# Re-annealing the table that orders an attention and feed-forward kernel, from the second batch on

## The chip, the cores and the metric

The kernel runs on one core of one Trainium2 chip. The metric is the device time of one execution in microseconds (us); a smaller time is better. The engines are called PE (TensorE, matmul), DVE (VectorE), ACT (ScalarE), POOL (GpSimd) and SP (SyncE, which here only issues transfers). PSUM has eight banks, which hold the results of matmuls.

## The reference

Eight batches of eight heads with 576 tokens of 64 go through linear attention with an exponential feature map; the result, 4608 tokens of 512, goes through a gated feed-forward layer.

```
phi(x):  p = x @ w_phi;  p = p - max|p|;  concat(exp(p), exp(-p))     # 128 -> 256 features
kv = sum_s phi(k)_s v_s ;  z = sum_s phi(k)_s
num / (phi(q) . z + 1e-6)   with  num = phi(q) @ kv
x = attention output as [4608, 512]
out = (relu(x @ w_gate) * (x @ w_val)) @ w_out                        # 512 -> 1536 -> 512
```

Inputs and output are float32; the products run in bfloat16.

## The kernel before

The whole kernel is one hand-made schedule. `ORDER` is a table of 2343 words. A word is `name.args:banks@slot`: the name of a step, its indices (batch or token group, chunk, head group), the PSUM banks that it uses and, where it opens a new buffer of a ring, which one. The last loop of the kernel walks the table and calls `do_<name>` for each word. Each engine carries out the steps that are its own strictly in the order of the table; a step on another engine is met only through the data, banks and buffers that they share.

The steps that the prediction speaks of, by batch `b` (attention) or token group `g` (feed-forward; group `g` below 8 is the first 512 tokens of batch `g`, group 8 holds the 64 leftover tokens of all batches):

- `kr` (PE, line 592) projects a third of the keys, 24 matmuls; `kx` (DVE, line 696) takes the largest absolute value; `ke` (ACT, line 688) the exponentials; `kv` (PE, line 794) sums keys by values, in products of 65 columns; `kc` and `kd` copy it from PSUM, on ACT or on DVE.
- `vs`, `vo` and `vq` (POOL, lines 745, 757 and 773) scale the values for `kv`.
- `qt` (DVE) transposes queries, `qc` (PE, line 854) projects them, `qx` and `qe` are their maximum and exponentials.
- `nu` (PE, line 917) makes the numerators, 65 columns; `nt`, `nv` and `nr` (DVE, lines 938, 948 and 956) scale and add them and take the reciprocal of the denominator; `nx` (POOL, line 960, writes `xu`) multiplies by it: one step for each 128 tokens of a batch.
- `xt` (SP, line 992) is a transposing transfer from `xu` into `xTs` (group 8: `xTm`). There are four for each group, and a group's first value or gate product needs all four.
- `fv` and `fg` (PE, line 1097) are value and gate products of one chunk of 128 of the 1536 columns, four matmuls of 512 columns each; `va` or `vb` (ACT or DVE) copy the value, `ga` (DVE, line 1118) applies the gate and writes `h`.
- `ps` (POOL, line 1337) makes half sums of `h`, and `fw` (PE, line 1361, 12 products of 256 columns) is the output product, in a form with seven products in place of eight; `ys` to `y4` add its parts; `ow` and others write to memory.
- `xs` (POOL, line 1169), `fi` (PE, line 1194) and their helpers do the same for the first products of groups 7 and 8; `xs` adds the token sums that `fi` multiplies.
- Loads: `lk`, `lq`, `lm` and `ln` (keys, queries and their leftover tokens) are issued by POOL (lines 464, 496, 508 and 514) in its own order, between its compute steps. `lv` and `lw` (values) and `xt` are issued by SP.

Batches overlap: while group 1 goes through its value and gate products, batch 2 is in its numerators and batch 3 in its projections. There is one buffer for loaded queries (`qn`) and one for keys (`kn`), four of `xu`, three of `u` and of `r`.

Of the kernel before, what the change touches and what calls it, by code (L numbers as in the profile page):

```python
# [53 lines left out]
vq.1.0 kr.1.2:5037 vq.1.1 pb.0.3:4 qx.1.0.2:6 kx.1.2.0:5@mk5 qe.1.0.1.1:1 va.0.10:2@val3
qe.1.0.1.0:1 qe.1.0.2.0:6 kv.1.1:4 mt.0 wo.1 kx.1.2.3:7 qy.1.0:2 kc.1.1:4@kv1 fg.0.9:1
ke.1.2.0.0:5@kp0 qz.1.0:2@my1 kx.1.2.1:0 kx.1.2.2:3 ke.1.2.3.1:7 ku.2@kT3 vo.1.0@vs4 ke.1.2.1.1:0
kk.1.2.0@ek4 qu.1.0@mz0 vs.1.0.1 kk.1.2.1 ke.1.2.3.0:7 fv.0.8:6 ga.0.9:1 ke.1.2.0.1:5 fg.0.10:4
lv.2.0 fg.0.8:2 va.0.8:6@val2 wo.2 kt.2.1@kT2 vs.1.0.0 ke.1.2.1.0:0 ga.0.10:4 vo.1.2@vs1 qw.1.0@cq1
vs.1.2.0 kt.2.0 vs.1.2.1 ke.1.2.2.0:3 mc.0:7156 ga.0.8:2 nu.1.2.1:0 ke.1.2.2.1:3 mx.0.3:6 kv.1.0:4
# [1418 lines left out]
```

## Time and profile before

| | us |
|---|---|
| runs of the kernel, median of 3 | 360.89 (360.67 to 361.22) |
| the profiled execution | 360.87 |
| its span (first to last instruction) | 359.1 |
| PE, POOL busy within the span | 352.9, 325.6 |
| DVE, ACT busy | 312.9, 235.8 |

The busy times are those of the profiled execution. Its span is what the rows of the trace add up to; the rest of its time, 1.8 us, lies around it. In rows of the trace the first number is the start in us from the start of the span, the second is the time from the first start to the last end of the instructions that the row groups (xN says how many), then the engine, the line of the kernel, the operation and output<-inputs; in square brackets stands how long the engine was idle before it and for whom it waited. SPq and POOLq mean that the row is the issue of a transfer, not the transfer. In a row on issues of transfers the last number is the median from issue to landing.

### The profile page before, as it was taken

How to read it: one execution, taken by the hardware profiler on the slowest of the kernel's cores; microseconds unless marked ns; L12 is line 12 of the kernel's file. 1: busy time of each engine (PE TensorE's matmuls, PEld its weight loads, DVE VectorE, ACT ScalarE, POOL GpSimd, SP SyncE). 2: the span in 40 equal slices, each digit the busy share in tenths (PEclk: the TensorE clock that was granted, in tenths of full speed). 3: DMA queues.
4: the chain of work that ended last, by engine and by line, in shares of the span. 5: the costliest groups of instructions: out<-in, count | busy, mean ns of one | idle time of the engine just before them, and what ended most of it. 6: DMA issues, size and time to landing. Idle time of an engine off the chain costs nothing.

```text
span 359.1 us, 10076 instructions
## 1 busy us (share of the span) xinstructions
PE 352.9 (98%) x3876; PEld 222.2 (62%) x3876; DVE 312.9 (87%) x721; ACT 235.8 (66%) x564; POOL 325.6 (91%) x393
## 2 busy tenths in 40 slices
PE   8999999999999999999999999999999999999996
PEld 6678966445575656765576546666656566444684
DVE  5999999989999999999997999999898853898744
ACT  3999996986698869786897269656861424454310
POOL 8674988999999999976999589989999999999994
PEclk9999999999999999999999999999999999999999
DMA  7999999990947494369215980778300221600017
GB/s 124 257 198 204 164 199 159 180 164 7 178 68 157 53 157 95 68 127 135 58 39 105 158 136 2 176 107 103 62 0 16 45 59 25 227 0 2 0 31 206
DMA packets 90770, 38.16 MB, mean 106 GB/s; under 512 B 64226, under 2 KB 86370, under 8 KB 90722
## 3 DMA queue, kind: packets, MB, share of 16 engines
q0 software_dynamic: 33504, 15.03, 32.5%
q1 hardware_dynamic: 56754, 21.83, 27.7%
q10 hardware_dynamic: 464, 0.66, 0.8%
q8 instruction: 30, 0.49, 0.6%
q14 instruction: 18, 0.15, 0.1%
HBM read 37.81 MB, written 9.44 MB: 132 GB/s over the span
## 4 chain that ended last, share of the span: by engine, by line
PE 85%; DVE 8%; ACT 2%; DMA 2%; issue 1%; POOL 1%; SPq 0%; DVEq 0%
PE bank L1097 35%; PE bank L1361 18%; PE bank L1194 10%; PE bank L794 5%; PE bank L1224 4%; PE bank L917 3%; PE bank L592 2%; PE bank L854 2%; PE bank L1256 2%; ACT kp L688 2%; DMA w64f<-in_w_phi_dram 2%; DVE t L938 1%; DVE u L948 1%; DVE h L1118 1%; DVE mk L696 1%
## 5 line engine op out<-in xcount | busy, mean ns | idle before, releaser
L688 ACT ACTIVATE kp<-bank 128x384 bf16<-128x384 f32 x192 | 84.2, 513 | 16.6 <-DVE mk L696 7.4
L1097 PE MATMUL bank<-xTs,wv 128*128 128x512 bf16 x304 | 75.7, 379 | 0.0
L1097 PE MATMUL bank<-xTs,wg 128*128 128x512 bf16 x304 | 74.6, 379 | 0.0
L869 ACT ACTIVATE qp<-bank 128x512 bf16<-128x512 f32 x128 | 69.9, 627 | 6.5 <-PE bank L854 4.2
L1118 DVE SCALAR_TENSOR_TENSOR h<-bank,val 128x512 bf16<-128x512 f32 x90 | 60.5, 680 | 6.7 <-PE bank L1097 4.5
L1112 ACT CAST val<-bank 128x512 bf16<-128x512 f32 x59 | 35.1, 594 | 33.4 <-PE bank L1097 30.4
L745 POOL TENSOR_TENSOR vs<-vn,ek 128x780 bf16<-128x780 f32 (+2 forms) x40 | 53.8, 1366 | 0.8 <-ACT ek L705 0.4
L696 DVE TENSOR_REDUCE mk<-bank 128x3 f32<-128x384 f32 x96 | 49.1, 542 | 0.2
L960 POOL TENSOR_TENSOR xu<-u,r 128x512 bf16<-128x512 f32 x36 | 37.4, 1045 | 11.6 <-DVE r L956 11.5
L1361 PEld LDWEIGHTS <-h 128*128 128x128 bf16 x432 | 41.1, 98 | 10.0 <-issue 2.6
L1097 PEld LDWEIGHTS <-wg 128*128 128x128 bf16 x304 | 27.8, 98 | 30.2 <-issue 1.3
L1097 PEld LDWEIGHTS <-wv 128*128 128x128 bf16 x304 | 27.6, 98 | 27.3 <-issue 0.9
L877 DVE TRANSPOSE_TENSOR_REDUCE maxq<-bank 128x16 f32<-128x512 f32 x56 | 36.9, 690 | 0.1
L948 DVE TENSOR_TENSOR u<-bank,t 128x195 f32<-128x195 f32 (+1 forms) x108 | 32.9, 327 | 1.8 <-POOL xu L960 0.9
L1361 PE MATMUL bank<-wo,h 128*128 128x256 bf16 x260 | 32.5, 273 | 0.0
L1337 POOL TENSOR_TENSOR vs<-h 128x256 bf16<-128x256 bf16 x42 | 28.0, 671 | 3.7 <-DVE h L1118 3.6
L938 DVE TENSOR_TENSOR t<-bank,cq 128x195 f32<-128x195 f32 (+1 forms) x96 | 29.6, 326 | 1.9 <-PE bank L917 1.2
L917 PEld LDWEIGHTS <-qp 128*128 128x128 bf16 x512 | 23.1, 98 | 10.2 <-issue 0.5
L1337 POOL TENSOR_TENSOR h<-h,vs 128x256 bf16<-128x256 bf16 x44 | 28.6, 676 | 0.0
L1337 POOL TENSOR_TENSOR vs<-vs,h 128x256 bf16<-128x256 bf16 x42 | 28.0, 672 | 0.6
L1337 POOL TENSOR_TENSOR h<-h 128x256 bf16<-128x256 bf16 x42 | 27.9, 674 | 0.3
L917 PE MATMUL bank<-kv,qp 128*128 128x65 bf16 x512 | 26.0, 193 | 0.2 <-ACT kv L805 0.2
(156 smaller groups left out, 686.0 us busy)
## 6 DMA issues: line engine op xcount, KB each, us to landing
vn<-in_v_dram SPq DMA_DIRECT2D x24, 256.0 KB, 4.3
out_dram<-xTs SPq DMA_DIRECT2D x17, 256.0 KB, 3.0
kn<-in_k_dram POOLq DMA_DIRECT2D x7, 512.0 KB, 8.1
qn<-in_q_dram POOLq DMA_DIRECT2D x7, 512.0 KB, 8.0
out_dram<-obp SPq DMA_DIRECT2D x14, 256.0 KB, 2.6
wv<-in_moe_w_val_dram POOLq DMA_DIRECT2D x3, 512.0 KB, 9.4
wg<-in_moe_w_gate_dram POOLq DMA_DIRECT2D x3, 512.0 KB, 8.8
wo<-in_moe_w_out_dram POOLq DMA_DIRECT2D x3, 512.0 KB, 8.3
```

The costliest lines, as they stand in the source:

```text
L688: nc.scalar.activation(kp_of(3 * b + j)[:, i, s].rearrange("p n f -> p (n f)"), bank[bk[0]][:, 0 : 3 * F], AF.Exp, scale=(1.0, -1.0)[s],)
L696: nc.vector.tensor_reduce(mk_of(3 * b + j)[:, :, i], bank[bk[0]][:, 0 : 3 * F].rearrange("p (n f) -> p n f", f=F), axis=AX.X, op=ALU.max, ...
L745: nc.gpsimd.tensor_tensor(vs_of(3 * b + j)[:, s, 0:n].rearrange("p n i e -> p (n i) e")[:, :, 0:e], src[:, lo:hi].rearrange("p h i e -> p ...
L869: nc.scalar.activation(qp_of(4 * b + i)[:, s, 4 * hq : 4 * hq + 4].rearrange("p h m -> p (h m)"), bank[bk[0]], AF.Exp, scale=(1.0, -1.0)[s],)
L877: nc.vector.tensor_reduce((maxq0[:, i] if b == 0 else maxq)[:, :, i, 4 * hq : 4 * hq + 4].rearrange("p t h -> p h t"), bank[bk[0]].rearran ...
L917: nc.tensor.matmul(bank[bk[0]][:, E * n : E * (n + 1)], lhsT=qp_of(4 * b + i)[:, s, h, :], rhs=kv_of(b)[:, h, s, 0:E],)
L948: nc.vector.tensor_tensor(u_of(serial(b, i))[:, lo:hi], parts(bk, n)[:, :, 0], t_of(3 * serial(b, i) + g)[:, 0:n], op=ALU.add,)
L960: eng.tensor_tensor(xu_of(n).rearrange("p (h d) -> p h d", d=D), u_of(n)[:, :, 0:D], r_of(n).to_broadcast([P, H, D]), op=ALU.mult,)
L1097: nc.tensor.matmul(bank[bk[0]], lhsT=w[:, dc, P * f : P * f + P], rhs=xT(g)[:, dc, :], start=(dc == 0), stop=(dc == NDC - 1),)
L1118: nc.vector.scalar_tensor_tensor(h2_of(g, f), bank[bk[0]], 0.0, val_of(NFC * g + f), op0=ALU.max, op1=ALU.mult)
L1337: eng.tensor_tensor(sum_of(g, n, j), a, b, op=op)
L1361: nc.tensor.matmul(bank[bk[0]][:, col : col + HN], lhsT=x[:, P * u : P * (u + 1)], rhs=w, start=(n in (1, 5, 6) and u == us[0] and j == 0) ...
```

## The change

Only the table changes. Its first 297 words, up to 39.08 us of the profiled execution (batch 1's first value and gate products for group 0), are the same. Behind them the same steps stand in another order, with other banks and other ring buffers, found by annealing on a model in which transfers land later than the trace had them. Three copies from PSUM go from ACT to DVE and three others from DVE to ACT (three `vb` became `va`, three `kc` became `kd`). The transfers on SP (113 words) keep their order among themselves, and so do the loads on POOL (54 words). But POOL's loads stand at other places between POOL's compute steps. Two lines of the diff:

```
-qc.3.1:4305 qx.3.1.3:5 qx.3.1.0:4 vs.3.1.0@vs2 ps.1.4.3 lq.4.2 xt.2.2 kk.3.2.0 vq.3.0@vr0 ps.1.4.2
+nr.8.0@r0 ku.4@kT2 y3.1:2 xt.2.3 lq.4.2 xt.2.2 od.0.0 fv.2.2:4 qe.3.1.1.1:6 qe.3.1.1.0:6
```

POOL before, at the last two normalisations of batch 2 (line 960, `nx.2.3` and `nx.2.2`) and the q load of batch 4 (line 496):

```order
92 L960 TENSOR_TENSOR xu_135<-u_127,r_131 128x512
93 L960 TENSOR_TENSOR xu_136<-u_128,r_132 128x512
94 L1337 TENSOR_TENSOR h_152<-h_152 128x256 x4
95 L1337 TENSOR_TENSOR h_152<-h_152,vs_98 128x256
96 L745 TENSOR_TENSOR vs_99<-vn_75,ek_94 128x12x65
97 L1337 TENSOR_TENSOR h_152<-h_152,vs_98 128x256
98 L496 DMA qn_73<-in_q_dram 128x8x256
```

POOL now, at the same place:

```order
97 L960 TENSOR_TENSOR xu_135<-u_127,r_131 128x512
98 L1337 TENSOR_TENSOR h_152<-h_152 128x256
99 L960 TENSOR_TENSOR xu_136<-u_128,r_132 128x512
100 L496 DMA qn_73<-in_q_dram 128x8x256
101 L745 TENSOR_TENSOR vs_99<-vn_75,ek_93 128x8x65 x2
102 L773 TENSOR_TENSOR vr_102<-vm_76,ek_93 64x8x65
103 L1337 TENSOR_TENSOR h_152<-h_152,vs_98 128x256 x2
```

The seven pieces of compute between the second normalisation and the load have moved elsewhere; the load follows it at once.

DVE before, at the reciprocal that `nx.2.2` waits for (the last line 956 here; line 696 is the absolute maximum of batch 3's keys):

```order
150 L956 RECIPROCAL r_130<-u_127 128x8
151 L696 TENSOR_REDUCE mk_85<-bank_65 128x3
152 L948 TENSOR_TENSOR u_128<-bank_69,t_126 128x195
153 L938 TENSOR_TENSOR t_125<-bank_63,cq_116 128x195
154 L948 TENSOR_TENSOR u_128<-bank_66,t_124 128x130
155 L948 TENSOR_TENSOR u_128<-bank_63,t_125 128x195
156 L956 RECIPROCAL r_131<-u_128 128x8
157 L696 TENSOR_REDUCE mk_85<-bank_67 128x3
```

DVE now:

```order
149 L696 TENSOR_REDUCE mk_85<-bank_68 128x3
150 L956 RECIPROCAL r_130<-u_127 128x8
151 L696 TENSOR_REDUCE mk_85<-bank_63 128x3
152 L938 TENSOR_TENSOR t_125<-bank_64,cq_116 128x130
153 L938 TENSOR_TENSOR t_126<-bank_69,cq_116 128x195
154 L948 TENSOR_TENSOR u_128<-bank_64,t_125 128x130
155 L948 TENSOR_TENSOR u_128<-bank_69,t_126 128x195
156 L696 TENSOR_REDUCE mk_85<-bank_67 128x3
157 L956 RECIPROCAL r_131<-u_128 128x8
158 L696 TENSOR_REDUCE mk_85<-bank_70 128x3
```

Three of the absolute maxima now stand ahead of that reciprocal, where one stood.

POOL before, from the last two normalisations of batch 7 (line 960) to the first token sum (line 1169):

```order
259 L960 TENSOR_TENSOR xu_135<-u_129,r_132 128x512
260 L1337 TENSOR_TENSOR vs_100<-h_152 128x256
261 L960 TENSOR_TENSOR xu_134<-u_128,r_131 128x512
262 L1337 TENSOR_TENSOR vs_98<-vs_100,h_152 128x256
263 L1337 TENSOR_TENSOR vs_100<-h_152 128x256
264 L1337 TENSOR_TENSOR h_152<-h_152 128x256
265 L1337 TENSOR_TENSOR vs_100<-h_152 128x256
266 L1337 TENSOR_TENSOR vs_98<-vs_100,h_152 128x256 x2
267 L1337 TENSOR_TENSOR h_152<-h_152 128x256
268 L1169 TENSOR_TENSOR qT_108<-xTs 128x512
```

POOL now:

```order
266 L960 TENSOR_TENSOR xu_136<-u_128,r_132 128x512
267 L1337 TENSOR_TENSOR vs_100<-h_152 128x256
268 L1337 TENSOR_TENSOR vs_99<-vs_100,h_152 128x256
269 L1337 TENSOR_TENSOR h_152<-h_152,vs_97 128x256
270 L1142 TENSOR_TENSOR wv<-wv 128x512
271 L1337 TENSOR_TENSOR h_152<-h_152 128x256 x2
272 L1337 TENSOR_TENSOR vs_99<-vs_100,h_152 128x256
273 L960 TENSOR_TENSOR xu_135<-u_127,r_130 128x512
274 L1337 TENSOR_TENSOR vs_100<-h_152 128x256 x2
275 L1337 TENSOR_TENSOR h_152<-h_152 128x256 x2
276 L1337 TENSOR_TENSOR vs_99<-vs_100,h_152 128x256 x2
277 L1169 TENSOR_TENSOR qT_108<-xTs 128x512
```

The normalisation ahead of the last one has moved up: seven pieces lie between them, where one lay. Seven pieces lay between the last one and the token sum, and six do now.

More of the change, by code (lines that the diff above doesn't have):

```diff
@@ L54 @@
[L54 to L59, printed above, removed]
@@ new lines @@
+fg.1.6:1 qx.2.0.2:2 qx.2.0.0:5 fg.1.3:4 fv.1.4:3 ga.1.6:1@hs12 ga.1.3:4@hs15 ke.2.2.3.0:6
+kk.2.2.1@ek0 kk.2.1.0@ek1 ke.2.2.3.1:6 va.1.4:3@val1 kk.2.1.1 qe.2.0.2.0:2@qp0 qx.2.0.3:7
+qe.2.0.1.0:0 lq.3.2 lv.2.2 lw.2.1 od.0.2 od.0.3 mn.0.1:5 mn.0.0:1 mn.0.2:4 qe.2.0.3.0:7
+nt.8.0.0:1@t0 kk.2.2.0 nt.8.0.2:4@t1 nv.8.0.0:1@u2 kt.3.2@kT1 fv.1.8:6 fv.1.0:3 nv.8.0.2:4 tw.2.0
+vb.1.8:6@val2 qc.2.1:1074 qe.2.0.2.1:2 va.1.0:3@val3 qe.2.1.0.1:1 vq.2.0@vr1 qe.2.1.0.0:1 fg.1.0:2
+kt.3.1@kT2 vs.2.0.1@vs2 vs.2.0.0 vq.2.1 fv.1.11:6 qx.2.1.1:0 qx.2.1.2:7 qx.2.1.0:1 vs.2.2.0@vs0
@@ new lines @@
+nt.2.3.2:3@t3 lv.3.3 lw.3.0 qt.3.1@qT0 lv.3.1 nv.2.3.2:3@u0 kx.3.1.1:7@mk4 nt.2.2.1:2@t2 fg.1.1:5
+ga.1.1:5@hs5 kx.3.1.0:0 kx.3.1.3:1 fv.1.9:3 kx.3.1.2:4 fg.1.7:6 nu.2.3.1:5 nt.2.3.1:5@t1
+ke.3.1.1.1:7 kk.3.0.0@ek2 ke.3.1.1.0:7 nu.2.3.0:7 nt.2.3.0:7@t0 va.1.9:3@val2 ke.3.1.3.0:1 kk.3.0.1
+ke.3.1.2.1:4 fg.1.9:3 ga.1.7:6@hs6 nv.2.3.1:5 nv.2.3.0:7 ga.1.9:3@hs7 ps.1.3.2 ps.1.3.5 ps.1.2.5
+ps.1.2.4 nx.2.0@xu1 ps.1.1.1 ps.1.2.1 fw.1.1:1 ps.1.1.3 ps.1.2.3 ke.3.1.0.1:0 ys.1:1 nu.2.2.2:4
+nu.2.2.0:0 kr.3.2:6573 ke.3.2.3.1:3@kp3 ke.3.2.1.0:5 nr.2.3@r1 nt.2.2.2:4@t3 nv.2.2.1:2@u1
@@ new lines @@
+ps.2.1.5 ps.2.2.5 kx.4.2.0:3 ke.4.2.2.0:2@kp3 kx.4.2.1:4 fv.2.8:0 fg.2.6:6 vb.2.8:0@val1
+ga.2.6:6@hs0 fg.2.8:7 ga.2.8:7@hs4 fw.2.1:1 ku.5@kT2 mn.1.0:0 mn.1.1:6 kk.4.1.1 kt.5.0 mw.1@cm1
+kx.4.2.2:2 ke.4.2.3.0:5 ke.4.2.0.0:3 ps.2.1.0 ke.4.2.3.1:5 ps.2.1.2 ps.2.2.2 ke.4.2.1.1:4
+ke.4.2.1.0:4 ke.4.2.0.1:3 qc.4.0:5437 ys.2:1 fw.2.2:1 vs.4.0.0@vs0 nt.8.1.1:6@t1 nt.8.1.0:0@t2
+ps.2.2.0 nv.8.1.0:0@u0 ps.2.3.2 vs.4.0.1 ps.2.4.0 ps.2.3.0 qe.4.0.1.1:4@qp0 qx.4.0.0:5 qt.5.1@qT0
+qe.4.0.1.0:4 ke.4.2.2.1:2 qe.4.0.2.0:3@qp2 qx.4.0.2:3 qe.4.0.0.0:5@qp4 nv.8.1.1:6 qx.4.0.1:4
@@ new lines @@
+qx.4.0.3:7 fw.2.5:0 fw.2.6:2 yw.2:2 kv.4.0:6 fv.3.5:4 ps.2.3.5 vb.3.5:4@val2 qe.4.0.0.1:5 y2.2:1
+qe.4.0.3.0:7@qp3 qe.4.0.2.1:3 qe.4.0.3.1:7 kc.4.0:6@kv1 fw.2.7:2 mn.1.2:5 qc.4.1:1374 ps.2.4.3
+ps.2.4.1 vs.4.1.1@vs1 ps.2.4.5 ps.2.4.2 qe.4.1.3.0:4 kk.4.2.1@ek1 fv.3.0:6 va.3.0:6@val3 yz.2:2
+fw.2.4:2 nt.8.1.2:5@t0 y1.2:0 qx.4.1.1:3 ln.2.0 ps.2.4.4 vs.4.1.0 qx.4.1.2:7 qx.4.1.3:4 qx.4.1.0:1
+nv.8.1.2:5 kt.5.2@kT3 y3.2:2 qe.4.1.1.1:3 qe.4.1.1.0:3 qe.4.1.2.1:7 fv.3.6:6 fw.2.3:0 y4.2:0
+kk.4.2.0 qe.4.1.2.0:7 qe.4.1.3.1:4 va.3.6:6@val0 qe.4.1.0.0:1 kr.5.0:3574 vs.4.2.0@vs3
@@ new lines @@
+kx.5.1.3:0 nu.4.3.0:5 nt.4.3.0:5@t3 nv.4.3.0:5 nr.4.2@r0 ke.5.1.3.0:0 ke.5.1.3.1:0 fv.3.8:2 fg.3.2:1
+nu.4.3.2:5 ga.3.3:6@hs3 fv.3.7:0 va.3.7:0@val3 ps.3.1.5 ps.3.2.5 ke.5.1.2.0:7 vb.3.8:2@val1
+nt.4.3.2:5@t0 nv.4.3.2:5 kx.5.1.1:4 fg.3.8:6 ga.3.8:6@hs9 ow.2.2 kr.5.2:2504 fg.3.10:7
+ke.5.2.0.1:2@kp3 ke.5.2.0.0:2 ke.5.1.0.1:3 kx.5.2.1:5@mk4 ga.3.2:1@hs10 ga.3.10:7@hs13 fg.3.7:6
+fv.3.9:1 ke.5.2.2.1:0 ke.5.2.2.0:0 ke.5.2.1.0:5 ke.5.1.0.0:3 vq.5.0 ps.3.3.5 ke.5.2.1.1:5
+va.3.9:1@val1 fv.3.1:7 va.3.1:7@val2 ps.3.3.0 nx.4.2@xu2 vs.5.0.1@vs2 ga.3.7:6@hs15 vs.5.0.0
@@ new lines @@
+kx.5.2.2:0 kx.5.1.0:3 ps.3.1.4 ps.3.1.2 ps.3.2.2 ps.3.3.2 ps.3.3.4 kx.5.2.3:4 kk.5.1.0@ek3
+ke.5.2.3.1:4 nr.4.3@r1 kx.5.2.0:2 fg.3.1:6 qc.5.0:0531 ga.3.1:6@hs0 kk.5.2.0@ek4 ke.5.2.3.0:4
+ps.3.2.4 ps.3.1.1 qe.5.0.2.0:3@qp0 qe.5.0.3.1:1@qp4 qe.5.0.3.0:1 qx.5.0.1:5 fg.3.9:7 ga.3.9:7@hs2
+qe.5.0.1.1:5@qp2 qe.5.0.1.0:5 fw.3.1:2 qx.5.0.3:1 kt.6.0@kT2 kv.5.0:6 qx.5.0.0:0 kd.5.0:6@kv0
+qc.5.1:4715 qx.5.1.3:5 qx.5.1.2:1 ys.3:2 kk.5.1.1 qe.5.0.0.1:0@qp3 qe.5.0.0.0:0 fw.3.2:2
+qe.5.1.1.1:7 nx.4.3@xu1 ps.3.2.1 ps.3.1.3 ps.3.2.3 ps.3.3.1 qx.5.1.1:7 fw.3.6:6 qe.5.1.3.0:5
@@ new lines @@
+va.4.10:7@val2 qw.5.0@cq1 ke.6.0.0.1:1@kp0 ke.6.0.0.0:1 ps.3.4.2 nx.8.1@xu0 ps.3.4.1 ps.3.4.5
+vs.5.2.0@vs3 ps.3.4.3 ps.3.4.0 kx.6.0.3:0@mk0 vs.5.2.1 kv.5.2:7 kx.6.0.1:3 ke.6.0.1.1:3 ke.6.0.1.0:3
+ke.6.0.3.0:0 ke.6.0.2.0:2 ke.6.0.3.1:0 ps.3.4.4 fw.3.3:4 nu.5.3.0:3 kx.6.0.0:1 nt.5.0.0:5@t2
+ke.6.0.2.1:2 kd.5.2:7 nv.5.0.0:5@u2 nt.5.0.1:6@t1 nv.5.0.1:6 nu.5.0.2:1 nt.5.0.2:1@t3 y4.3:4
+fg.4.1:7 nu.5.1.1:5 nu.5.1.0:0 fv.4.7:6 ga.4.1:7@hs5 kx.6.0.2:2 fg.4.3:4 nu.5.3.1:7 kt.6.1@kT3
+nt.5.3.0:3@t0 nt.5.1.1:5@t2 nv.5.1.1:5@u1 fv.4.3:2 kk.6.0.1@ek5 va.4.7:6@val1 va.4.3:2@val3
@@ new lines @@
+nv.5.0.2:1 nr.5.0@r0 nt.5.1.0:0@t1 nv.5.3.0:3@u0 lk.7.3 nx.5.0@xu3 lm.7.0 nu.5.1.2:6 fg.4.0:5
+ga.4.3:4@hs8 nu.5.2.0:1 nu.5.2.1:2 fg.4.7:3 nu.5.3.2:4 nv.5.1.0:0 nt.5.2.0:1@t2 nt.5.1.2:6@t3
+nt.5.3.1:7@t0 nv.5.1.2:6 nt.5.3.2:4@t1 nv.5.3.1:7 nr.5.1@r1 lq.6.2 nx.5.1@xu2 ow.3.3 fv.4.11:0
+nu.5.2.2:6 va.4.11:0@val0 nv.5.3.2:4 lw.6.1 xt.5.0 lv.6.0 ow.2.1 lm.7.1 xt.5.1 lv.6.3 fg.4.10:7
+nv.5.2.0:1@u2 nr.5.3@r2 nx.5.3@xu1 xt.5.3 lv.6.1 lv.6.2 ga.4.7:3@hs11 nt.5.2.1:2@t3 nv.5.2.1:2
+nt.5.2.2:6@t0 ga.4.10:7@hs0 fv.4.9:4 nv.5.2.2:6 nr.5.2@r0 fv.4.0:1 vb.4.0:1@val3 ga.4.0:5@hs3
@@ new lines @@
+nt.7.3.2:5@t1 nu.7.1.2:3 fv.6.2:2 nv.7.3.2:5 ga.6.7:7@hs12 nt.7.2.0:0@t2 nt.7.1.2:3@t3 ps.5.2.5
+wt.2.1.0 ps.5.2.3 fw.5.6:1 nu.7.2.1:5 fv.6.8:7 nv.7.1.2:3 nv.7.2.0:0@u0 ps.5.4.0 ps.5.3.2
+wt.4.1.0@kp2 wt.4.0.0 ps.6.1.3@vs3 ps.6.3.3 ps.5.4.1 ps.5.4.4 ps.5.3.5 ps.5.3.3 nt.7.2.1:5@t1 mt.3
+nv.7.2.2:4 yw.5:1 ps.6.1.1 nv.7.2.1:5 nr.7.2@r0 fv.6.0:3 nu.7.0.0:0 vb.6.2:2@val3 nt.7.0.0:0@t3
+nx.7.2@xu1 ps.6.2.3@vs2 ps.5.4.5 nr.7.1@r1 nx.7.1@xu0 ps.5.4.2 wt.3.0.0 nr.7.3@r2 vb.6.8:7@val1
+nt.7.0.1:6@t2 fg.6.8:4 nu.7.0.2:5 nt.7.0.2:5@t0 fw.5.7:1 fw.5.5:2 fg.6.2:7 yz.5:1 nx.7.3@xu3
@@ new lines @@
+fi.0.5.1:4 fi.0.11.1:5 fi.0.10.2:0 ps.8.1.0 ps.7.1.1 ps.8.1.1 iq.0.10:6@u2 ia.0.5:46
+iv.0.10.0:7@val2 ga.8.10:0@hs11 fi.0.10.7:3 fi.0.4.7:1 ps.7.1.0 ps.8.3.2 ga.8.4:2@hs14 fi.0.5.5:7
+fi.0.5.2:4 fi.0.5.6:6 ia.0.11:50 iq.0.5:7@u0 iv.0.4.1:1@val0 fi.0.4.4:1 fi.0.11.5:2 ps.8.1.4
+ps.8.3.4 ps.8.2.4 ps.7.3.0 iv.0.10.1:3@val3 ga.7.4:1 ib.0.5:67 fi.0.5.3:7 ps.8.3.3 iv.0.5.0:7@val2
+ga.8.5:4@hs0 ps.8.2.1 ps.8.3.0 fi.0.5.7:6 fi.0.11.6:0 ib.0.11:01 iq.0.11:2@u1 fi.0.10.4:3 ps.8.3.1
+fi.0.11.2:5 fi.0.11.3:1 iv.0.5.1:6@val1 ga.7.10:3@hs4 ps.7.1.4 fw.8.1:7 ys.8:7 iv.0.11.0:1@val0
@@ new lines @@
+ga.8.11:5@hs5 ps.8.2.2 ps.8.1.5 ps.8.2.0 ps.8.2.5 fi.0.5.4:6 fi.0.11.7:0 fw.8.2:7 ga.7.5:6
+iv.0.11.1:0@val2 fi.0.11.4:0 fw.8.6:4 yw.8:4 ga.7.11:0@hs7 ps.8.3.5 ps.7.2.0 ps.8.4.0 ps.8.4.5
+ps.8.4.4 fw.8.5:2 fw.8.7:4 yz.8:4 fw.7.1:3 y1.8:2 fw.8.4:4 ps.7.1.5 ps.7.2.1 ps.7.2.4 ps.8.4.1
+ps.7.2.5 ow.5.1 fw.7.6:1 ps.8.4.2 y2.8:7 ys.7:3 ps.8.4.3 yw.7:1 y3.8:4 fw.8.3:2 y4.8:2 fw.7.2:3
+ps.7.3.2 ps.7.3.4 ps.7.3.1 ps.7.3.5 fw.7.7:1 fw.7.5.1:5 fw.7.5.0:6 ps.7.4.2 ps.7.4.1 ps.7.4.4
+ps.7.4.0 ps.7.4.3 ps.7.4.5 yz.7:1 fw.7.4:1 y1.7.0:6 y1.7.1:5 y3.7:1 fw.7.3.0:6 y4.7.0:6 fw.7.3.1:5
```

394 lines of the change are left out of this document (167 added, 227 removed).

## The prediction

> **What bounds the kernel now.** I read the page first (busy shares, the chain that ended last), then busy time by stretch, the waits, and then transfers and timelines around the places where the order moves a load.
>
> ```profile
> span 359.1 us, 10076 instructions
> PE 352.9 (98%) x3876; PEld 222.2 (62%) x3876; DVE 312.9 (87%) x721; ACT 235.8 (66%) x564; POOL 325.6 (91%) x393
> PEclk9999999999999999999999999999999999999999
> PE 85%; DVE 8%; ACT 2%; DMA 2%; issue 1%; POOL 1%; SPq 0%; DVEq 0%
> ```
>
> TensorE is busy for 98% at full clock, and 85% of the chain is its own. The next view cuts the span behind the first word that moves; column two is the length, then PE, weight loads, DVE, ACT, POOL with their counts.
>
> ```profile
> 58.25:109.91 51.66, 51.36 (x601) 29.20 (x599) 50.10 (x126) 41.35 (x104) 51.09 (x53) 1.00 0.83 125
> 109.91:154.40 44.49, 44.45 (x536) 27.72 (x533) 42.47 (x98) 34.56 (x82) 44.00 (x54) 1.00 0.64 106
> sum 316.16, PE 315.40 PEld 193.88 DVE 278.10 ACT 202.97 POOL 297.69; mean PE 45.06 PEld 27.70 DVE 39.73 ACT 29.00 POOL 42.53
> ```
>
> The sum row is 39.08 to 355.24 us, from the first moved step to the start of the last matmul. From 58 to 154 us POOL is as full as PE (95.1 of 96.2 us): two engines bound that stretch, and PE alone the rest.
>
> How much can any order win? The first three of these rows (of the chain) give undisturbed spacings: 0.216 us for a product of 512 columns, 0.030 for 65, 0.110 for 256. The other two (of PE's timeline) are a key and a query projection.
>
> ```profile
> 110.07 4.32 PE bank L1097 x20
> 222.18 1.52 PE bank L794 x50
> 339.71 15.82 PE bank L1361 x144
> 153.95 0.52 PE L592 MATMUL bank<-w,kT 32*128 32x128 bf16 x24
> 107.75 0.68 PE L854 MATMUL bank<-qT,w 32*128 32x512 bf16 x8
> ```
>
> Behind 39.08 us the order holds 824 products of 512 columns (178.0 us), 672 of 256 (73.9), 1136 of 65 (34.1), 19 key projections at 0.52 and some 0.03 of switching (10.5), 13 query projections at 0.68 (8.8), and small ones for which I estimate 7: 312.3 of the 316.2 us. So PE loses about 4 us there, and no order of these steps gains more: 357 us is the floor.
>
> **The change part by part.** The work is the same. Each of the 19 and 13 projections, the products and the copies has the duration of its row wherever it stands; three PSUM copies going each way between ACT and DVE cancel. What can change is only PE's 4 us of loss: what waits vanish and what waits come. I went through the order for each transfer that follows a POOL step, since the DMA words keep their order on SP and among themselves on POOL, while POOL's loads are moved against its compute.
>
> *The place where a load moves.* In the order before, the q load of batch 4 stands five pieces behind the normalisation of batch 2's last two tiles. In the new one it stands directly behind the last of them, so it starts when the transpose of that tile does. Rows of before:
>
> ```profile
> 104.34 2.56 SPq L992 DMA_TRANSPOSE xTs<-xu  x2
> 101.87 2.04 POOL L960 TENSOR_TENSOR xu<-u,r 128x512 bf16<-128x512 f32 x2
> 109.07 0.93 POOL L496 DMA_DIRECT2D qn<-in_q_dram  x1
> 109.91 1.89 PE L1097 MATMUL bank<-xTs,wv 128*128 128x512 bf16 x8
> qn<-in_q_dram POOLq DMA_DIRECT2D x1, 512.0 KB, 6.2
> ```
>
> The two normalisations end at 103.9, the last two transposes issue back to back from 104.34 (the second at about 105.7), the load at 109.07 (landing after 6.2), the first product of batch 2 at 109.91. The landing of the second transpose, asked for alone, is:
>
> ```profile
> xTs<-xu SPq DMA_TRANSPOSE x1, 2.4
> ```
>
> It landed at 108.1, 1.8 us ahead of its use, and the load was issued after that. Now what these transposes cost where a load was issued with them; the answers for 236.0 to 236.5 and 160.4 to 160.9 us, with the issues:
>
> ```profile
> qn<-in_q_dram POOLq DMA_DIRECT2D x1, 512.0 KB, 9.2
> xTs<-xu SPq DMA_TRANSPOSE x1, 7.5
> 236.41 1.23 SPq L992 DMA_TRANSPOSE xTs<-xu  x1
> 236.32 0.97 POOL L496 DMA_DIRECT2D qn<-in_q_dram  x1
> kn<-in_k_dram POOLq DMA_DIRECT2D x1, 512.0 KB, 8.4
> xTm<-xu SPq DMA_TRANSPOSE x1, 7.5
> 160.57 1.51 SPq L992 DMA_TRANSPOSE xTm<-xu  x1
> 160.76 0.95 POOL L464 DMA_DIRECT2D kn<-in_k_dram  x1
> ```
>
> Twice a load within 0.2 us of the transpose, twice 7.5 us in place of 2.4, and the load itself ends later still. A third, with the k load 3.4 us ahead of it (57.33 against 60.75), took 5.6:
>
> ```profile
> xTs<-xu SPq DMA_TRANSPOSE x1, 5.6
> 57.33 0.92 POOL L464 DMA_DIRECT2D kn<-in_k_dram  x1 [1.30 <-DVE t L938]
> 60.75 1.34 SPq L992 DMA_TRANSPOSE xTs<-xu  x1
> ```
>
> All of these happened where nobody needed the tile soon. In the new order PE meets it at once: the words ahead of batch 2's first value product are the same number of each kind as before (16 value, 16 gate, 24 numerator, 7 key and 5 query projections and so on), so PE arrives at about 109.9 again. The load may be issued up to 1 us ahead of the transpose, since SP first issues the transpose before it. DVE adds to that: the reciprocal that the normalisation waits for has moved behind two more absmax reductions, by 0.48 us each (five in 2.38 us):
>
> ```profile
> 102.27 0.16 DVE L956 RECIPROCAL r<-u 128x8 f32<-128x8 f32 x1
> 102.35 2.38 DVE L696 TENSOR_REDUCE mk<-bank 128x3 f32<-128x384 f32 x5
> ```
>
> So it ends near 103.3 to 103.8, the normalisation (1.0) near 104.4 to 104.9, and the transpose is issued between 105.0 and 106.2; I take 105.7, as before. Its latency lies between 2.4 (no effect) and 8.0 (7.5 and the spread of the twins). The nearest rows are the twins' 7.5; the twin at 236 had two more transposes behind it, and here only an output follows, and the same q load alone took 6.2 at 109 us, so I take 6.8. The tile is there at 112.5, and the product starts 2.6 us later than at 109.91. **Term one: +2.6**, from 0 (no effect) to +4.3 (106.2 and 8.0).
>
> [...]
>
> *What that delay gives back.* While PE stands, POOL works on, so what PE lost behind POOL from 109.91 to 154.40 us is gone. The stretch holds 108 products of 512 columns (23.3), 96 of 256 (10.5), 206 of 65 (6.2), 4 key (2.2) and 2 query projections (1.4) and by my estimate 0.5 of small ones: 44.1 of 44.49 us. **Term two: -0.4.** Of POOL's pieces ahead of the late products, two groups:
>
> ```profile
> L745 POOL TENSOR_TENSOR vs<-vn,ek 128x780 bf16<-128x780 f32 (+2 forms) x40 | 53.8, 1366 | 0.8 <-ACT ek L705 0.4
> L1337 POOL TENSOR_TENSOR vs<-h 128x256 bf16<-128x256 bf16 x42 | 28.0, 671 | 3.7 <-DVE h L1118 3.6
> ```
>
> If POOL's cover is gone instead, because its half sums need the late products, this is 0: ahead of the first of them stand six pieces of line 745 (1.37) and six half sums (0.67), 12.2 us of POOL's work, more than PE's delay.
>
> *A wait that goes.* The token sum of batches 6 and 7 waited on a transpose that SP issued late, being in others until 287.9:
>
> ```profile
> 290.56 1.16 POOL L1169 TENSOR_TENSOR qT<-xTs 128x512 bf16<-128x512 bf16 x1 [0.68 <-DMA xTs<-xu]
> 292.40 1.48 PE L1361 MATMUL bank<-wo,vs 128*128 128x256 bf16 x12 [0.22 <-POOL vs L1337]
> 293.72 1.47 PE L1361 MATMUL bank<-wo,h 128*128 128x256 bf16 x12
> 295.39 1.48 PE L1361 MATMUL bank<-kp,vs 128*128 128x256 bf16 x12 [0.20 <-POOL vs L1337]
> ```
>
> PE lost 0.22 there and 0.35 later (1.67 from 293.72 to 295.39, against 12 x 0.110 = 1.32). In the new order the normalisations of the two tiles whose transposes held SP stand further ahead, and six half sums (6 x 0.67 = 4.0 us) lie between the last normalisation and the token sum, more than an undisturbed 2.4. **Term three: -0.6**, from -0.6 to 0.
>
> *The rest.* From 154 to 290 us PE loses 1.2 us by the same count of spacings, in many small pieces. Nothing in the new order takes a known one away; I take 0, with 0.6 either way.
>
> Sum: +2.6 - 0.4 - 0.6 + 0 = +1.6 on the profiled execution. That took 360.87 us (span 359.1 and 1.8 around it), as good as the median of 360.89: **362.5 us**.
>
> **The rivals.** Two rows bear on them, one of the transfers (the median of all 28 of this form) and PE's longest wait on another engine behind 39 us.
>
> ```profile
> xTs<-xu SPq DMA_TRANSPOSE x28, 2.5
> PEld L1361 <- POOL vs L1337: 1.4, 4, 0.5
> ```
>
> (1) *The landing isn't late* (faster, the other side). If the transpose lands within 4.2 us, by 109.9, term one is 0 and the sum is -1.0, or -1.4 if POOL's stretch stays as good without PE's delay: 359.5 to 359.9. For it speaks that the 28 transposes of this form have a median of 2.5; against it, that all three near a load took 5.6 or more. It decides at a latency of 5.2 (109.9 + 1.0): below that the change gains. [...] (3) *PE's clock falls*. A PE that stands for 2.6 us or more might lose its clock for a while. Every slice of before shows 9, and the longest of PE's waits on another engine behind 39 us is 0.5, so no row prices it; if PE ran at half speed for as long as it had stood, it would lose 1.3 more: 363.8.
>
> [...] (4) *The change does nothing*: the moved steps are all covered and PE's losses only change places, 360.6 to 361.2; this would need term one near +1, and I count it with (2).
>
> **How the numbers follow.** My forecast (a late landing, 361.6 to 363.6) has 0.43; rival 3, and a landing or a new wait that is worse, 0.11; rivals 2 and 4 together 0.17; rival 1 has 0.29. A measurement of this kernel tells about 0.2%, 0.7 us, from no change. Slower than 361.6: 0.43 + 0.11 = 0.54. Within 360.2 to 361.6: 0.17. Faster: 0.29. Forecast alone: 361.6 to 363.6. The range takes in the middle of rival 1 (359.6) and most of rival 3: 359.6 to 364.6.
>
> **What would show it.** In the profile of the changed kernel: the transpose issued at 105 to 106.2 us lands after 6 to 8 us, and a row of PE at line 1097 near 112 carries a wait of some 2.5 us on a transfer of xu; POOL has idle time behind it or PE no more waits until 154; the token sum near 292 has no wait on a transfer; PE's clock is 9 in each slice. The prediction is wrong if that transpose lands within 4 us, if the load isn't in flight with it, or if a wait of a microsecond or more stands at a place not named here.

## The result, and the profile after

| | us |
|---|---|
| the changed kernel, median of 4 runs | 372.19 (370.53 to 374.71) |
| the kernel before, on the same chip, median of 4 | 360.78 (360.01 to 361.22) |
| ratio to before | 1.0325, 95% interval 1.026 to 1.0389 |
| profiled execution and its span | 374.71, 372.9 |

The change makes the kernel 11.4 us slower, not 1.6. The four runs of the changed kernel differ by 4 us, and their mean granted clocks (the share of its full clock that PE was given) differ with them: 0.979 in the 374.71 us run, 0.986, 0.988 and 0.995 in the 370.53 us run. The profile is that of the slowest, 13.8 us over the profiled 360.87 of before.

Of its page, the span, PE and its clock in 40 slices of 9.3 us, and the chain:

```profile
span 372.9 us, 10026 instructions
PE 355.2 (95%) x3827; PEld 223.2 (60%) x3876; DVE 312.3 (84%) x721; ACT 234.5 (63%) x564; POOL 325.7 (87%) x393
PEclk9999999999996999999999996999999999999998
PE 76%; POOL 7%; DMA 6%; issue 3%; DVE 3%; ACT 3%; SPq 1%; POOLq 0%; ACTq 0%
```

In before, each slice had clock 9 and PE was 85% of the chain. Now two slices have 6, and transfers and POOL are in the chain. PE's waits from 39 us on:

```profile
PE bank L1097 <- DMA xTs<-xu: 8.2, 3, 3.7
PE bank L794 <- POOL vs L745: 0.2, 1, 0.2
```

Three waits on transposes, 8.2 us; before had none. PE's timeline shows where (first value products of groups 2, 4 and 5), and the table by stretches gives the clock behind the two long ones (the column behind POOL's):

```profile
112.96 0.61 PE L1097 MATMUL bank<-xTs,wv 128*128 128x512 bf16 x1 [3.70 <-DMA xTs<-xu]
114.64 3.62 PE L1097 MATMUL bank<-xTs,wg 128*128 128x512 bf16 x8
189.67 1.02 PE L1097 MATMUL bank<-xTs,wv 128*128 128x512 bf16 x3 [0.77 <-DMA xTs<-xu]
225.16 1.89 PE L1097 MATMUL bank<-xTs,wv 128*128 128x512 bf16 x4 [3.68 <-DMA xTs<-xu]
...
113.06:119.60 6.54, 6.32 (x32) 2.62 (x34) 0.51 (x1) 2.79 (x6) 6.52 (x8) 0.59 0.43 113
225.27:231.90 6.63, 6.63 (x39) 3.35 (x39) 0.41 (x1) 2.51 (x6) 6.63 (x8) 0.56 0.01 2
```

Eight gate products took 3.62 us at 114.64; undisturbed, eight take 1.89 (a row of e1 below). With 0.59 and 0.56 of the clock granted, the two slow stretches lost 6.54 x 0.41 = 2.7 and 6.63 x 0.44 = 2.9 us. Each of these two windows takes in an edge at full clock. Cut finer, the granted clock is 0.50 from 111.6 to 118.4 and from 224.3 to 231.1 us, 6.8 us each time, and 1.00 right before and behind. It fell while PE stood, 2.3 and 2.8 us into the two waits. Waits and clock together: 3.70 + 3.68 + 0.77 + 2.7 + 2.9 = 13.75, about the 13.8 by which this execution is longer.

The place that the prediction named, as it came out (transfers first, then the issues on POOL and SP):

```profile
qn<-in_q_dram POOLq DMA_DIRECT2D x1, 512.0 KB, 9.5
xTs<-xu SPq DMA_TRANSPOSE x1, 7.1
...
105.70 0.94 POOL L496 DMA_DIRECT2D qn<-in_q_dram  x1
104.18 2.80 SPq L992 DMA_TRANSPOSE xTs<-xu  x2
```

The load was issued at 105.70, the second transpose at 105.79; the transpose took 7.1 us in place of 2.4, landed at 112.9, and PE's product started at once. The load landed later still, at 115.2. What was late was the transpose's completion and not its data: between 106.6 and 108.3 us SP's queue moved 512 packets and 0.13 MB, which is the whole tile (128 x 512 numbers of two bytes). From 108.3 to 111.0 it moved 26 packets of almost no bytes, while 651 of the load's went; of the 1040 that POOL's queue moved from 106.6 to 115.2, 979 had gone by 112.9.

The place that it did not name is at group 5: three loads of POOL stand between the normalisations of batch 5, and a fourth right ahead of them.

```profile
205.70 0.96 POOL L464 DMA_DIRECT2D kn<-in_k_dram  x1 [6.46 <-DVE t L938]
207.84 0.75 POOL L508 DMA_DIRECT2D km<-in_k_dram  x1
208.59 0.91 POOL L496 DMA_DIRECT2D qn<-in_q_dram  x1
210.69 0.75 POOL L508 DMA_DIRECT2D km<-in_k_dram  x1
...
214.10 5.47 SPq L992 DMA_TRANSPOSE xTs<-xu  x1
220.93 1.91 SPq L992 DMA_TRANSPOSE xTs<-xu  x1
...
xTs<-xu SPq DMA_TRANSPOSE x1, 9.6
xTs<-xu SPq DMA_TRANSPOSE x1, 8.0
```

The transposes issued at 210.8 and 214.1 took 9.6 and 8.0 us. The issue of the one at 214.1 held SP for 5.47 us in place of 1.3, so the last one, whose tile was ready at 216.6, was issued only at 220.93. In before the same k and q loads were issued at 193.1 and 194.8, six microseconds ahead of the first of these transposes, and the third one, issued at 208.8, took 3.1:

```profile
194.76 0.92 POOL L496 DMA_DIRECT2D qn<-in_q_dram  x1
xTs<-xu SPq DMA_TRANSPOSE x1, 3.1
```

### The profile page after: what moved, and what is told of

Read it like the earlier page. It is cut to its first block, busy times and chain, and to the rows that moved or that the text cites. A ratio compares the mean times of both kernels' runs of the same rounds, so it can differ in the third digit from the quotient of the medians.

```text
span 372.9 us, 10026 instructions
## 1 busy us (share of the span) xinstructions
PE 355.2 (95%) x3827; PEld 223.2 (60%) x3876; DVE 312.3 (84%) x721; ACT 234.5 (63%) x564; POOL 325.7 (87%) x393
## 4 chain that ended last, share of the span: by engine, by line
PE 76%; POOL 7%; DMA 6%; issue 3%; DVE 3%; ACT 3%; SPq 1%; POOLq 0%; ACTq 0%
PE bank L1097 28%; PE bank L1361 18%; PE bank L1194 10%; PE bank L794 4%; DMA xTs<-xu 4%; PE bank L1224 4%; PE bank L917 3%; ACT kp L688 2%; DMA vm<-in_v_dram 2%; PE bank L592 2%; POOL vs L1337 2%; PE bank L455 2%; PE bank L854 2%; POOL vs L745 2%; PE bank L1256 2%
## 5 line engine op out<-in xcount | busy, mean ns | idle before, releaser
L1097 PE MATMUL bank<-xTs,wg 128*128 128x512 bf16 x288 | 77.7, 393 | 0.7
L1112 ACT CAST val<-bank 128x512 bf16<-128x512 f32 x62 | 36.4, 595 | 55.7 <-PE bank L1097 39.6
L917 PE MATMUL bank<-kv,qp 128*128 128x65 bf16 x512 | 25.0, 193 | 0.3 <-ACT kv L805 0.2
```

What stands on the lines that cost most here:

```text
L917: nc.tensor.matmul(bank[bk[0]][:, E * n : E * (n + 1)], lhsT=qp_of(4 * b + i)[:, s, h, :], rhs=kv_of(b)[:, h, s, 0:E],)
L1097: nc.tensor.matmul(bank[bk[0]], lhsT=w[:, dc, P * f : P * f + P], rhs=xT(g)[:, dc, :], start=(dc == 0), stop=(dc == NDC - 1),)
```

## The experiments

Theory A: a POOL load that is in flight when a transpose is issued holds back its landing; PE, which needs the tile at once, stands; and where it stands as long as here (3.70 and 3.68 us) it loses its clock on top. Rival B: the tiles come late by the order of DVE and POOL, and the loads are innocent. Rival C: the clock falls for a reason of its own. In e1 to e4 the table fills fewer lines of the file, so their line numbers are 13 lower (12 in e4): L1084 and L1085 are line 1097.

**e1: the q load of batch 4 three POOL steps later.**

```
-xt.2.3 lq.4.2 xt.2.2
+xt.2.3 xt.2.2
...
-vq.3.0@vr0
+vq.3.0@vr0 lq.4.2
```

> The changed kernel with one word moved: the q load of batch 4 (lq.4.2) stands three POOL steps later, behind vq.3.0. Theory A (that load, in flight with the transpose xt.2.2, holds back its landing, and the idle PE then loses clock): xt.2.2 lands about 2.5 us after its issue, near 108.3; the wait of 3.7 us at fv.2.2 is gone, so is the slow clock behind it (2.6 us); some 366 us in place of 372.2. Rival B (tiles are late by the order of DVE and POOL, loads don't matter): the wait stays, 372. Rival C (the clock falls whatever PE waits for): the wait goes and the slow clock stays at that place, 368.5.

Measured: 366.64 us (ratio to before 1.016, 1.0119 to 1.0202), against 1.0325 for the changed kernel. The transpose, and PE at group 2 and at group 5:

```profile
xTs<-xu SPq DMA_TRANSPOSE x1, 2.4
...
109.47 1.03 PE L1084 MATMUL bank<-xTs,wv 128*128 128x512 bf16 x3
110.33 1.89 PE L1084 MATMUL bank<-xTs,wg 128*128 128x512 bf16 x8
218.60 1.76 PE L1084 MATMUL bank<-xTs,wv 128*128 128x512 bf16 x4 [3.23 <-DMA xTs<-xu]
```

At the first place the latency is back at 2.4, there is no wait, and PE runs at full speed (eight gate products in 1.89 us). The second place keeps a wait of 3.23 us, and the clock's mean is 0.62 from 218.5 to 223.0 us. B and C fail here: one moved load takes away wait and slow clock.

**e2: the q load of batch 6 earlier, where POOL stood idle.**

```
-ps.3.4.4
+ps.3.4.4 lq.6.2
...
-lq.6.2 nx.5.1@xu2
+nx.5.1@xu2
```

> The changed kernel with one word moved: the q load of batch 6 (lq.6.2) is issued ahead of the k load of batch 7 (lk.7.3), where POOL stands idle for 6 us, in place of between the normalisations of batch 5. Theory A: with one 512 KB load less in flight from 208 to 219 us, the transposes of batch 5 land in 3 to 5 us, the last by 221; the wait of 3.7 us at fv.5.8 and the slow clock behind it (2.6 us) go; some 366 us in place of 372.2. Rival B: the transposes stay late because nx.5.2 is late; 372. If the k load alone holds them back, the wait only shrinks, to about 2 us, and the clock stays up: 368.

Measured: 367.10 us (1.0179, 1.0148 to 1.021).

```profile
221.12 1.04 PE L1084 MATMUL bank<-xTs,wv 128*128 128x512 bf16 x4
223.48 0.28 PE L781 MATMUL bank<-vs,kp 128*128 128x65 bf16 x4 [0.46 <-POOL vs L732]
```

The wait of 3.68 is gone, with the slow clock; what stays is 0.46 us for the values of batch 6, whose loads share the same time. A k load is still there, and the transpose issued at 210.4 took 6.3 us. But the product that needs all four tiles started at 221.12 without a wait, in place of 225.16 behind one. B fails here too.

**e3: both moves.**

> Both moves together. Theory A: both waits and both stretches of slow clock go, about 13 us: 359 to 361.5, within 0.3% of the kernel before. Rival B: 372. If one wait only moves on to the next transpose, 363 to 366.

Measured: 362.82 us (1.0057, 1.0038 to 1.0075). From 372.19, e1 takes 5.6, e2 5.1 and both 9.4 of the 11.4 us; the two places add up to 10.7, so they are nearly independent. 2.2 us stay over before (360.64), more than the expectation had.

**e4: the early load in the kernel before.** The expectation speaks of a place behind ps.1.3.1. In the kernel that ran, the load stood directly behind nx.2.2, as in the changed kernel, and was issued at 103.77, ahead of both transposes.

```
-nx.2.2@xu3
+nx.2.2@xu3 lq.4.2
...
-ps.1.4.3 lq.4.2 xt.2.2
+ps.1.4.3 xt.2.2
```

> The kernel before with one word moved: lq.4.2 stands behind ps.1.3.1, so it is issued near 105.8 us, with xt.2.2 (105.7), in place of 109.1. Theory A: xt.2.2 lands after 7 us in place of 2.4, near 112.8; PE waits 2.9 us at the first value product of batch 2; later waits give back 0.4: 363.3 if PE keeps its clock, up to 365.5 if it loses it. Rival B: the transposes are as early as before, so nothing changes: 360.8.

Measured: 362.00 us over 10 runs (1.0047, 1.0023 to 1.007); nine lie between 361.2 and 363.2 at clocks of 0.998 to 1.0, one, the profiled one, has 365.23 at 0.993. Its rows, the last two transposes first:

```profile
xTs<-xu SPq DMA_TRANSPOSE x1, 8.4
xTs<-xu SPq DMA_TRANSPOSE x1, 7.4
...
112.71 0.61 PE L1085 MATMUL bank<-xTs,wv 128*128 128x512 bf16 x1 [2.20 <-DMA xTs<-xu]
...
112.80:117.00 4.20, 3.98 (x12) 1.56 (x14) 1.72 (x4) 2.31 (x5) 4.17 (x3) 0.61 0.14 31
```

One moved load, with nothing else changed, makes 8.4 and 7.4 us of 2.5 and gives PE a wait of 2.2. The second transpose was issued 1.5 us behind the load. Behind the wait the clock's mean was 0.61 from 112.8 to 117.0 us in this execution: six value products from 113.54 took 2.70 us, four gate products from 116.08 again 1.03. If it was 0.50 while it was low, that makes some 3.3 us (4.2 x 0.39 / 0.50, an estimate). The other nine were not traced, so how long PE waited in them isn't known; their clocks show no such loss. Their median is 361.9, 1.2 us over before, where the expectation had 2.5 for a kept clock. Whether their waits were shorter or later waits gave more back is open.

**e5: PE kept busy in the two waits.** The words are an idle-filler that the kernel already uses at its start.

```
-fv.2.2:4
+zz.28:4 fv.2.2:4
...
-fv.5.8:6
+zz.28:6 fv.5.8:6
```

> The changed kernel, and in each of its two long waits (ahead of fv.2.2 and of fv.5.8) PE does 28 products of zeros of 256 columns (3.1 us) into the bank that the next product overwrites; all else stays. Theory A1 (the idle PE is what costs the clock): the two transposes land as late as before and PE's next real product starts at the same time, but the clock stays up, so some 5 us of the profiled 374.7 go, to 369.5; every run near that, the scatter of 370.5 to 374.7 gone. Rival C (the clock falls for another reason, such as the transfers' load or heat): 372 with the same scatter. If the added products cost time themselves: over 372.

Measured: 370.30 us (1.0269, 1.0254 to 1.0284); the four runs lie within 369.66 to 370.89, at clocks of 0.997 and 0.998.

```profile
110.29 3.22 PE L455 MATMUL bank<-zero 128*128 128x256 bf16 x28
114.88 1.89 PE L1097 MATMUL bank<-xTs,wg 128*128 128x512 bf16 x8
...
113.00:119.00 6.00, 5.44 (x45) 2.91 (x45) 2.44 (x5) 3.83 (x8) 5.92 (x6) 1.00 0.49 149
222.00:229.00 7.00, 5.79 (x83) 3.49 (x83) 1.89 (x3) 3.47 (x8) 6.71 (x7) 1.00 0.00 0
```

At group 2 the last two transposes still took 4.8 us in the median, as in the changed kernel (2.5 and 7.1 there), and 3.6 us lie between PE's last real product and its next at 114.0. But the clock is 1.00 behind both waits, and the scatter shrinks from 4.2 to 1.2 us. The transfers are the same, so it is the idle PE that costs the clock here. With the clock kept the kernel is still 9.6 us slower than before (360.67). The added products save 1.9 us in the median, and 4.1 between the two profiled executions (374.71 and 370.60).

**e6: the normalisation nx.4.3 two steps earlier, on top of e3.**

```
-nr.4.3@r1
+nr.4.3@r1 nx.4.3@xu1
...
-nx.4.3@xu1 ps.3.2.1
+ps.3.2.1
```

> Both loads moved as in e3, and the normalisation nx.4.3 two POOL steps earlier (right behind its reciprocal). In e3 PE waited 0.69 us on the transpose of that tile at fv.4.4. Theory (what is left of the loss in e3, 2.2 us over the kernel before, is waits for tiles that come late by the order itself): xt.4.3 is issued 1.2 us earlier, the wait goes, 0.7 to 0.9 us less than e3: 362.0. Rival: POOL's displaced half sums make PE wait as long; 362.8.

Measured: 362.24 us (1.0044, 1.0029 to 1.0058); the interval overlaps that of e3. The profile shows the wait of 0.69 at fv.4.4 gone, and another in its place:

```profile
183.39 1.89 PE L1097 MATMUL bank<-xTs,wv 128*128 128x512 bf16 x7
84.02 0.28 PE L794 MATMUL bank<-vs,kp 128*128 128x65 bf16 x4 [0.86 <-POOL vs L745]
78.43 1.06 POOL L773 TENSOR_TENSOR vr<-vm,ek 64x520 bf16<-64x520 f32 x1 [1.06 <-DMA vm<-in_v_dram]
```

The second looks like a third collision: the q load of batch 3 (lq.3.2), issued at 71.7 here and at 74.03 in before, with a load of values whose issue holds SP from 69.39 to 72.14 in the changed kernel. POOL waited for the values until 78.4 here; in before they had landed at 75.0, 4.6 us behind their issue. It does not strike each time: in the profile of e7, with the q load at 71.45, POOL took them at 77.20 and nobody waited.

**e7: the loads of batch 6's values ahead of batch 5's transposes, on top of e6.**

```
-lw.6.1 xt.5.0 lv.6.0
+lw.6.1 lv.6.0 lv.6.3 lv.6.1 lv.6.2 xt.5.0
...
-xt.5.1 lv.6.3
+xt.5.1
...
-xt.5.3 lv.6.1 lv.6.2
+xt.5.3
```

> As e6, and the four loads of batch 6's values (lv.6.x) are issued ahead of batch 5's transposes on SP, right behind lw.6.1, in place of between them. Theory: the transposes then meet one k load only and xt.5.2 isn't held up on SP, and the values are there when POOL wants them, so the waits at fv.5.8 (0.4 to 0.6) and at kv.6.0 (0.5 to 0.8) go: 1.2 us less than e6, 360.8, level with the kernel before or better. Rival: the values themselves then collide with the k load, no change against e6.

Measured: 361.83 us over 12 runs (1.0032, 1.0009 to 1.0056), which the intervals don't tell from e6, and with a scatter from 359.63 to 364.25. The gain of 1.2 us that was expected isn't shown. Its profiled run is the fastest and has none of the waits at groups 4 and 5.

**e8: term three alone.** The kernel before, with one transpose of batch 7 issued ahead of an output and of its neighbour.

```
-ow.5.2 xt.7.3 xt.7.2
+xt.7.2 ow.5.2 xt.7.3
```

> The kernel before with one transfer moved on SP: xt.7.2, whose tile is ready before that of xt.7.3, is issued ahead of it and of an output. This measures term three of the prediction by itself. By the prediction: xt.7.0 is issued some 1.3 us earlier, the token sum doesn't wait, and PE gains 0.6 us: 360.0 against 360.6. Rival: the output products wait on POOL's half sums all the same, no change.

Measured: 359.48 us (0.997, 0.9959 to 0.998), all seven runs between 359.37 and 360.09.

```profile
289.11 1.15 POOL L1169 TENSOR_TENSOR qT<-xTs 128x512 bf16<-128x512 bf16 x1
291.39 1.48 PE L1361 MATMUL bank<-wo,vs 128*128 128x256 bf16 x12
294.02 1.47 PE L1361 MATMUL bank<-kp,vs 128*128 128x256 bf16 x12
```

In before, the three like rows (290.56, 292.40 and 295.39, in the prediction) carried waits; now none does. By the medians the gain is 1.2 us (360.67 to 359.48), twice what was expected, and this version is faster than both kernels.

**e9: the q load of batch 3 two steps later, on top of e7.**

```
-lq.3.2 tw.2.0 vq.2.0@vr1
+tw.2.0 vq.2.0@vr1 lq.3.2
```

> As e7, and the q load of batch 3 (lq.3.2) two POOL steps later, behind vq.2.0: near 74.1 us, as in the kernel before, in place of 71.4, where a load of values (lw.2.1) was still being issued. In e5 and e6 lw.2.1 landed at 78.3 in place of 75.4 and PE waited 0.9 to 1.3 us for POOL behind it; in the profile of e7 it did not, and the runs of e7 scatter from 359.6 to 364.3. Theory: that landing is the scatter; without it all runs lie near the lowest of e7, 359.6 to 360.3. Rival: the scatter has another cause and stays, median 361.8.

Measured: 360.62 us over 12 runs (1.0007, 0.9994 to 1.0019), from 360.03 to 361.83. The scatter shrinks from 4.6 to 1.8 us, close to the 1.6 of before measured beside it, and the median is level with before, but not in the range given. In the profiled execution (361.69 us) a wait on POOL's half sums is now the largest:

```profile
143.89 1.48 PE L1361 MATMUL bank<-kp,vs 128*128 128x256 bf16 x12 [0.82 <-POOL vs L1337]
```

Five moves (two loads at the large waits, one normalisation, one group of value loads, one more load) give the whole loss back. Each of the small three lies within the intervals of its neighbour, and only their sum, 362.82 to 360.62, is clear.

**e10: half of the load at the same place.**

```
-xt.2.3 lq.4.2 xt.2.2
+xt.2.3 lq.4.0 xt.2.2
...
-vq.3.1
+lq.4.1 vq.3.1
```

> The changed kernel with the q load of batch 4 in halves: heads 0 to 3 (256 KB) where the load stood, with xt.2.2, heads 4 to 7 three POOL steps later. If the transpose's landing waits for as much of the load as is in flight (theory A in its strict form): xt.2.2 lands 4 to 5 us after its issue in place of 7.1, the wait at fv.2.2 is 1 to 2 us in place of 3.7, the clock stays there; 367.5. If the second half delays it all the same: 7 us, no change, 372. If the mere presence of a POOL load costs a fixed 5 us: 372.

Measured: 368.50 us (1.0218, 1.0198 to 1.0238). Load and transpose, and PE:

```profile
qn<-in_q_dram POOLq DMA_DIRECT2D x1, 256.0 KB, 5.1
xTs<-xu SPq DMA_TRANSPOSE x1, 5.2
...
110.99 1.04 PE L1097 MATMUL bank<-xTs,wv 128*128 128x512 bf16 x4 [1.79 <-DMA xTs<-xu]
...
110.99:116.00 5.01, 5.01 (x41) 2.65 (x42) 3.21 (x6) 3.85 (x8) 4.86 (x5) 1.00 0.71 137
```

With half the load, the transpose took 5.2 us in place of 7.1, and the load 5.1; both were issued between 105.6 and 105.8, so they landed within some 0.3 us of each other. So the delay grows with the bytes of the load ahead, as far as two sizes show it. Behind the wait of 1.79 the clock was 1.00 in this execution. The second half stood behind five POOL steps and not three; in the changed kernel these end at 111.0, about when the transpose landed here. The time is 1 us above the expectation; the waits at groups 4 and 5 were still there.

**e11: the load one step later.**

```
-xt.2.3 lq.4.2 xt.2.2
+xt.2.3 xt.2.2
...
-vs.3.0.1@vs2
+vs.3.0.1@vs2 lq.4.2
```

> The changed kernel with the q load of batch 4 one POOL step (1.05 us) later, behind vs.3.0.1, so that it is issued near 106.8, 1 us behind xt.2.2. If the transpose only waits for what stands in the DMA engines ahead of it: it lands near 108.5 to 109 and the wait goes, 366.6 as e1. If the two share the engines from there on: 4 to 6 us, a wait of 1 to 2, 368 to 369. If the load counts as long as the transpose hasn't landed: 7 us, 372.

Measured: 367.66 us (1.0188, 1.0149 to 1.0227), level with e1 within the intervals. The load was issued between 107.2 and 107.4, the transpose between 106.3 and 106.5:

```profile
qn<-in_q_dram POOLq DMA_DIRECT2D x1, 512.0 KB, 8.3
xTs<-xu SPq DMA_TRANSPOSE x1, 2.4
```

The load issued some 0.9 us behind the transpose didn't touch it: 2.4 us, as without it. This is no test of two transfers that run together: in before, the first packets of this load show at 110.7 us, 1.6 us behind its issue at 109.07; by that they came near 108.9 here (an estimate), and the transpose had landed by then (106.5 and 2.4). That only what was issued ahead can delay a transfer isn't shown either: in e5 the values that SP began to issue at 69.3 to 69.5 landed after 9.1 us with the q load of batch 3 issued 2 us later (71.42), and after 6.5 in e9, with it at 73.94.

## Why the prediction was wrong

**Term one was right in place and cause, and near in size.** Issue forecast at 105.7, measured 105.79; latency 6.8, measured 7.1; landing 112.5, measured 112.9; the product moved from 109.91 to 112.96, 3.05 us against +2.6. PE came to it 0.65 us earlier than forecast (109.26), so the wait itself was 3.70. e1, e4, e10 and e11 show the cause. The tile's data had moved by 108.3 us and the landing came at 112.9, behind 979 of the 1040 packets on POOL's queue; by what mechanism it came so late no run shows. The 0.17 of rivals 2 and 4 would have needed a term near +1, at 105.7 a latency of some 5.2; the transpose took 7.1, and 5.2 only with half the load (e10).

**The step that failed is the walk through the order, "for each transfer that follows a POOL step".** It applied the collision to one place and not to the next, though the mechanism was the same. The prediction names group 5 nowhere. Its term for 154 to 290 us, "The rest", asks only which known waits go ("Nothing in the new order takes a known one away") and stands at 0, with 0.6 either way; it gives no reason why no wait should come. There the new order puts three POOL loads between the very normalisations that release group 5's transposes. PE waited 3.68 us for them and lost 2.9 to the clock in the profiled execution, and the place costs 5.1 us in the median (e2). This is also a sign that the prediction itself gave for being wrong: a wait of a microsecond or more at a place not named. Of the 2.2 us that e3 leaves, a late tile at group 4, the values of batch 6 and the third collision at 71 us are parts; e6, e7 and e9 take back the sum, and no run shows the share of each.

**The clock was left out of the sum.** Rival 3 named it, at 1.3 us, in a group that had a chance of 0.11 (with a worse landing and a new wait). The estimated wait of 2.6 was measured as 3.70, and the price as 2.7 and 2.9 us at the two places. The half speed, a supposition that no row of before showed, came as a granted clock of 0.50; but PE was held there for 6.8 us each time, not for as long as it had stood. The clock fell 2.3 and 2.8 us into the two long waits, and behind e4's wait of 2.2 us its mean was 0.61. Behind e10's 1.79 us it was 1.00, in the one execution that was profiled. What makes the runs scatter is not shown by itself; that it comes with the clock fits e5, where the slow clock is gone and the scatter falls from 4.2 to 1.2 us.

**Term two (-0.4)** was not seen alone. Its sign came: in the changed kernel PE waits for POOL nowhere between 114 and 154 us, and in e9, without the delay, it waits 0.82 there. Its size is below what these comparisons can tell.

**Term three (-0.6) had the right sign and mechanism.** In the changed kernel no token sum waits on a transfer; by itself, in the kernel before, the wait was worth 1.2 us (e8), twice the term. As a gain of the changed kernel it isn't shown: e9, with the collisions gone, is level with before and not faster.

**The bound held as far as was seen:** no version came under 357 us; the best median is 359.48.

**Slips in the working, none of which decides.** The q load stood seven pieces of POOL behind the last normalisation in before, as the listing of the order says, and not five. Rival 1 keeps the -0.4 of term two though it is what the delay gives back; without a delay the sum is -0.6, 360.3 us. The three copies each way between ACT and DVE are a net count: fifteen went each way, so they cancel all the same.

## What to carry to other kernels

When a schedule is moved, list for each transfer with a consumer behind it which loads are issued near it or ahead of it and not yet landed, on all queues, and price its landing up to theirs (in the changed kernel 112.9 against 115.2, in e10 within some 0.3 us); one collision found is a reason to look for all. Here a load did no harm behind the issue of the transfer (some 0.9 us later, 2.4 us to landing, e11), and little well ahead of it (14 us, 3.1 to landing, in before). In the two waits of 3.7 us here, 28 cheap products each kept the clock at 1.00 (e5). In the profiled execution here the clock cost 5.6 us beside 7.4 of the two waits; in the median, keeping it saved 1.9.

## What the runs showed of the hardware

A transpose of one 128x512 tile from SP, 2.4 us alone, took 7.1 us with a POOL load of 512 KB issued 0.1 us ahead of it, and 5.2 with 256 KB (e10); in the first case its data had moved 4.6 us before it counted as landed. In a crowded stretch the issue itself held SP: 5.47 us in place of 1.3, which delayed all that stood behind it in SP's order. PE's granted clock fell to 0.50 in the waits of 3.70 and 3.68 us and stayed there for 6.8 each time. Behind waits of 2.20 (e4, the one traced execution of ten) and 3.23 us (e1) its mean was 0.61 over 4.2 us and 0.62 over 4.5. Behind a wait of 1.79 (e10) it was 1.00 over 5.0.
